# Softmax weights and queries in two PSUM banks, six banks for matmuls, in a gated attention and Mish kernel

## The chip, the cores and the metric

The kernel runs on one core of a Trainium2 chip. The metric is the device time of one execution in microseconds (us). TensorE does the matmuls (PE in the profile's rows; PEld are its weight loads), VectorE (DVE), ScalarE (ACT) and GpSimd (POOL) the elementwise work, SyncE (SP) issues most DMAs.

## What is computed

A row of x (2048 rows of 640) is gated by its own sigmoid g between two branches: sliding, dilated attention over 8 keys with 32 heads of 20, and a two-layer MLP with Mish and 1728 hidden columns. All arrays are float32.

```python
g = sigmoid((x * gate_w).sum(-1, keepdims=True))
# A: W, dil = 8, 2; key and value rows pos, pos-2, ..., pos-14 (masked below 0)
logits = einsum("bhsd,bhswd->bhsw", q, kg) * Dh ** -0.5
attn = softmax(where(mask, logits, -1e9))
a = einsum("bhsw,bhswd->bhsd", attn, vg).transpose(...).reshape(B, S, D) @ wo
# B
h = einsum("bsd,df->bsf", x, w1) + b1
b = einsum("bsf,fd->bsd", h * tanh(softplus(h)), w2)
return g * a + (1 - g) * b
```

## The kernel before

**Matmuls.** Every float32 operand of a matmul is split into a rounded high part (ScalarE, a copy to fp32r) and the low rest, raw minus high (a subtraction on VectorE or GpSimd, `split`, line 348; its output is a tile called `pair`). A product is three matmuls (`mm3`, lines 394 to 396): high by high, high by low, low by high. For part of the weights, the rest is instead made by a DMA of GpSimd's queue that adds in memory (`split_added`, line 357). The second MLP layer and half of the output projection use a scheme with seven block products in place of eight; its sums of blocks are made on VectorE or GpSimd (`sums_of`, lines 751 and 764) or by accumulating DMAs of GpSimd's queue (lines 657 and 1066).

**Attention** is not done with matmuls. It works in 8 units (4 groups of 8 heads by 2 halves of the rows); `kv` holds keys and values of a unit, slot by slot, and `q` its queries. For two slots at a time VectorE multiplies q by the window of 8 keys (`scores`, line 451, into `pr`, 2560 elements in each partition), reduces over the 20 columns of a head (line 454), and after the softmax multiplies the values by the weights `pw` (`outputs`, line 488), and adds up over the 8 keys in three halving steps (lines 493, 494, 496). Softmax runs on four slots: maximum, subtraction, Exp on ScalarE (line 473), sum, reciprocal, gate, weights (line 482). Masks are small ScalarE copies (line 463). The result is transposed by 32-blocks on VectorE (line 407), stored, and read again as operand of the output projection.

**Stages.** q, k and v come from matmuls into PSUM that ScalarE copies out (lines 552, 554, 556); between the units' matmuls run those of the first MLP layer with Mish on ScalarE (line 669); then the second layer (`mlp2`), the output projection of the first half of the rows (`wo_first`), and that of the last two token blocks (`wo_second`). In `wo_second` a column block's matmuls come in two parts, an opening part over three row blocks of the operand and a closing one over two. When a group is done, VectorE adds the gated MLP result to the bank (`finish`, line 1282); the MLP results are gated by a multiplication (line 943), some after a load from memory.

**Order.** Nothing is left to run-time choice. Each step is a task with an engine, an estimated duration, a rank and buffers from rings (PSUM `bank`: 8, `pair`: 21, `raw` and others). `Plan.run` plays the tasks through with these estimates and writes the instructions of each engine in the order in which they start. Subtractions and sums marked "ANY" are done by GpSimd or VectorE: VectorE takes one only when it is due, GpSimd any that is ready. From the first attention task on, GpSimd may begin such a task only if it ends by `quiet`, the estimated end of a running score reduction; the instruction is then also made to wait (`follow`) for the VectorE instruction before that reduction:

```python
if on:
    fit = [t for t in fit if now + t.ns[0] <= quiet + 150 or t.rank <= -0.5]
```

Of the kernel before, what the change touches and what calls it, by code (L numbers as in the profile page):

```python
# [8 lines left out]
F32 = mybir.dt.float32  # L9
F32R = mybir.dt.float32r  # L10
AF = mybir.ActivationFunctionType
OP = mybir.AluOpType
AX = mybir.AxisListType
PSUM = bass.MemoryType.PSUM
DRAM = bass.MemoryType.DRAM

S, D, H, DH, W, F = 2048, 640, 32, 20, 8, 1728
KC = D // 128
NQ, HQ = 4, 8
QF = HQ * DH  # L20
# [6 lines left out]
BIG = 1e9  # L27
WARM, WARM_TAIL = 6, 4
WA = 256

# [27 lines left out]
class Plan:  # L60


    NEAR, PATIENCE = 8000, 2000

    LAG = {"PE": 220, "ACT": 220, "DVE": 200, "POOL": 150, "SP": 3000}
    FAR, ROOM = 25000, 5000
# [29 lines left out]
    def run(self):  # L96
        ready = {e: [] for e in self.LAG}
# [4 lines left out]
        quiet, gate, last, shared, begun = 0.0, None, None, [], False  # L102
# [33 lines left out]
        while left:  # L136
            again = not events or events[0][0] > now
            while again:
                again = False
                for e in self.LAG:  # L140
                    if busy[e]:
                        continue
                    fit = [t for t in ready[e] if fits(t)]
                    on = begun and loud
                    if e == "POOL":
                        fit += [t for t in shared if fits(t)]
                        if on:
                            fit = [t for t in fit if now + t.ns[0] <= quiet + 150 or t.rank <= -0.5]
                    elif e == "DVE":
                        fit += [t for t in shared if fits(t) and (not on or due(t))]  # L150
                    if not fit:
                        continue
                    t = min(fit, key=lambda t: t.key)
                    if t.both:
                        shared.remove(t)
                        t.eng = e
                    else:
                        ready[e].remove(t)
                    if type(t.ns) is tuple:
                        t.ns = t.ns[e == "DVE"]  # L160
                    for b in t.take:
                        b.ring.free -= 1
                        b.ring.at += 1
                        b.t = b.make()
                    t.start = now
                    ins = t.fn(e) if t.both else t.fn()
                    if e == "POOL" and on and quiet > now and gate and ins:
                        self.follow(ins, gate)
                    if e == "DVE":
                        if t.kind:  # L170
                            begun = True
                            loud -= 1
                        if t.kind == "qk sum":
                            quiet, gate = now + t.ns, last
                        last = ins or last
                    if e == "PE":
                        begun_pe = max(begun_pe, t.pos)
                    busy[e] = again = True
                    end = over = now + t.ns * self.CARE.get(e, 1.0)
                    heapq.heappush(events, (over, n, "idle", e))  # L180
                    if t.land:
                        wire = max(wire, end) + t.land
                        end = wire + (0 if e == "SP" else self.ADDING)
                    heapq.heappush(events, (end + self.LAG[e], n + 1, "done", t))
                    if e != "SP":
                        heapq.heappush(events, (over, n + 2, "own", t))
                    n += 3
            if not events:
                stuck = [(t.eng, t.rank, t.waits, getattr(t.fn, "__qualname__", "")) for e in ready for t in ready[e]]
                raise RuntimeError(f"nothing can go on at {now}, {left} left: {stuck[:20]}")  # L190
            now, _, what, x = heapq.heappop(events)
            if what == "idle":
                busy[x] = False
                continue
            if what == "ready":
                (shared if x.both else ready[x.eng]).append(x)
                continue
            if what == "done":
                left -= 1
                x.at = now  # L200
                for b in x.hold:
                    b.left -= 1
                    if not b.left:
                        b.ring.free += 1
                        if b.gone:
                            b.gone()
            for t in x.then:

                if (t.eng == x.eng and x.eng != "SP") != (what == "own"):
                    continue  # L210
                t.waits -= 1
                if not t.waits:
                    t.why, t.rdy = x, now
                    late = self.ROOM if x.eng == "SP" and t.eng == "ACT" and first[t] - begun_pe > self.FAR else 0
                    heapq.heappush(events, (now + max(t.late, late), n, "ready", t))
                    n += 1
# [4 lines left out]
def kernel(ctx: ExitStack, tc: tile.TileContext, x, wq, wo, w1, b1, w2, xt, gw, out):  # L221
    nc = tc.nc
    scale = DH ** -0.5
    V, G, A = nc.vector, nc.gpsimd, nc.scalar

    keep = ctx.enter_context(tc.tile_pool(name="keep", bufs=1))
    dram = ctx.enter_context(tc.tile_pool(name="dram", bufs=1, space=DRAM))
    psum = ctx.enter_context(tc.tile_pool(name="psum", bufs=8, space=PSUM))
    top = ctx.enter_context(tc.tile_pool(name="top", bufs=1, side="right"))
    pe = ctx.enter_context(tc.tile_pool(name="pe", bufs=1, side="right"))  # L230
    at = ctx.enter_context(tc.tile_pool(name="at", bufs=1))
# [1 line left out]
    NPAIR, NW, NRAW, NH = 21, 3, 7, 4  # L233
    def follow(ins, gate):
        tc.add_manual_dep(ins.ins, gate.ins.name,
                          mybir.DependencyInfo(mybir.DependencyClass.Sync, mybir.DependencyReason.DATA), reason="beside")

    plan = Plan({"bank": 8, "pair": NPAIR, "w": NW, "raw": NRAW, "raw1": 1, "hb": NH,
                 "ot": 1, "b": 11}, follow)

    def ps_buf():
# [23 lines left out]
    def act_ns(n):  # L265
        return 30 + 0.96 * n
# [13 lines left out]
    add = plan.add  # L280
# [36 lines left out]
    lg_w = lg.rearrange("p s h w -> p s w h")  # L317
    pw = at.tile([128, 8, W, HQ], F32, name="pw")
    pw_h = pw.rearrange("p s w h -> p s h w")
    pr = at.tile([128, 2, W, QF], F32, name="pr")  # L320
    mx = at.tile([128, 8, HQ], F32, name="mx")
    sm = at.tile([128, 8, HQ], F32, name="sm")
# [99 lines left out]
    def window(kv, s0, which):  # L422
        a = kv[:, s0:s0 + 9, which, :]
        return bass.AP(tensor=a.tensor, offset=a.offset, ap=[list(a.ap[0]), [ROW, 2], [ROW, W], [1, QF]])
# [6 lines left out]
    def attention(u, P, hq, ready, gates):  # L431


        kv, q = KV[UNIT[u]], Q[UNIT[u]]
# [13 lines left out]

        def scores(s0, rank, after):
            def mul():  # L450
                return V.tensor_tensor(pr, window(kv, s0, 0), q[:, s0:s0 + 2, None, :].to_broadcast([128, 2, W, QF]), op=OP.mult)  # L451

            def red():
                V.tensor_reduce(lg_w[:, s0:s0 + 2], pr.rearrange("p s w (h d) -> p s w h d", d=DH), op=OP.add, axis=AX.X)  # L454

            step = chain(rank)
            step("DVE", 2850, mul, ready[s0] + after, kind="qk")
            return step("DVE", 2750, red, kind="qk sum")

        def bounded(a, b, after):  # L460
# [15 lines left out]
        def shares(a, rank, e, copied):  # L476
            h = slice(a, a + 4)
            step = chain(rank)
            t = step("DVE", 415, lambda: V.tensor_reduce(sm[:, h], lg[:, h], op=OP.add, axis=AX.X), [e])
            step("DVE", 390, lambda: V.reciprocal(sm[:, h], sm[:, h]))  # L480
            step("DVE", 230, lambda: V.tensor_tensor(sm[:, h], sm[:, h], gate[:, P, h, None].to_broadcast([128, 4, HQ]), op=OP.mult), gates)
            return t, step("DVE", 430, lambda: V.tensor_tensor(pw[:, h], pw[:, h], sm[:, h, None, :].to_broadcast([128, 4, W, HQ]), op=OP.mult), [copied])

        def outputs(s0, rank, after):
            def mul():
                vw = window(kv, s0, 1)
                vw = bass.AP(tensor=vw.tensor, offset=vw.offset, ap=[list(d) for d in vw.ap[:3]] + [[DH, HQ], [1, DH]])
                V.tensor_tensor(pr.rearrange("p s w (h d) -> p s w h d", d=DH), vw,  # L488
                                pw[:, s0:s0 + 2, :, :, None].to_broadcast([128, 2, W, HQ, DH]), op=OP.mult)

            step = chain(rank)
            step("DVE", 2850, mul, after, kind="pv")
            step("DVE", 1495, lambda: V.tensor_tensor(pr[:, :, 0:4], pr[:, :, 0:4], pr[:, :, 4:8], op=OP.add), kind="pv")  # L493
            step("DVE", 855, lambda: V.tensor_tensor(pr[:, :, 0:2], pr[:, :, 0:2], pr[:, :, 2:4], op=OP.add), kind="pv")

            return step("DVE", 525, lambda: V.tensor_tensor(q[:, s0:s0 + 2], pr[:, :, 0], pr[:, :, 1], op=OP.add), kind="pv")
# [16 lines left out]
        for i, a in enumerate((4, 0)):  # L513
            h = 2 * u + i
# [938 lines left out]
```

## Time and profile before

| | us |
|---|---|
| timed runs | 632.35, 631.42, 631.64 |
| median | 631.64 |
| profiled execution: span from first to last instruction | 630.2 |
| busy TensorE, VectorE | 625.6, 581.0 |
| busy ScalarE, GpSimd | 333.5, 143.4 |

The profiled execution's own time is told by its span alone; the timed runs stand 1.2 to 2.2 us above that span. A row of the groups reads: line, engine, operation, output<-inputs by the program's names, shapes, count, then busy time in us and mean ns of one, then the engine's idle time just before and what ended it. A row of the timeline reads: start in us, duration in us, engine, line, operation, names, shapes, count, with the idle time before it in brackets. A row of the waits reads: who, for whom, us in total, times, the longest.

### The profile page before, as it was taken

What the parts mean: (1) busy time and instruction counts of PE and PEld (TensorE: products, weight loads), DVE (VectorE), ACT (ScalarE), POOL (GpSimd) and SP (SyncE); (2) the same over time, 40 slices, a digit from 0 to 9 for tenths busy, and PEclk for the clock granted to TensorE, in tenths of its full rate; (3) what the DMA queues carried; (4) which work ended last, traced back from release to release, by engine and by line L of the source; (5) the groups of instructions that cost most, each with busy time, mean ns of one, the idle gap of its engine ahead of it and who ended that gap; (6) DMA issues with size and microseconds to landing.
All of it is one profiled execution on the core that took longest, in us unless ns stands there. A gap on an engine that the chain in (4) does not pass through costs nothing.

```text
span 630.2 us, 8823 instructions
## 1 busy us (share of the span) xinstructions
PE 625.6 (99%) x2794; PEld 521.9 (83%) x2794; DVE 581.0 (92%) x610; ACT 333.5 (53%) x705; POOL 143.4 (23%) x154
## 2 busy tenths in 40 slices
PE   9999999999999999999999999999999999999997
PEld 6888888888888888888888888888888888888886
DVE  7699989999999998998999899999999989999934
ACT  6665764454536645353652626683765536666300
POOL 1321242232312332331333341211201010002320
PEclk9999999999999999999999999999999999999999
DMA  9999998999977998895898798899989867799985
GB/s 321 344 338 225 180 271 210 317 256 274 269 206 175 322 313 195 209 271 112 186 324 185 150 290 196 216 322 287 298 275 287 231 222 252 231 340 322 253 236 189
DMA packets 105694, 159.12 MB, mean 253 GB/s; under 512 B 13728, under 2 KB 52768, under 8 KB 105360
## 3 DMA queue, kind: packets, MB, share of 16 engines
q1 hardware_dynamic: 89648, 131.74, 64.1%
q0 software_dynamic: 15712, 26.56, 27.3%
q8 instruction: 22, 0.36, 0.2%
q10 hardware_dynamic: 288, 0.26, 0.1%
q14 instruction: 24, 0.20, 0.1%
HBM read 95.27 MB, written 67.51 MB: 258 GB/s over the span
## 4 chain that ended last, share of the span: by engine, by line
PE 98%; DMA 1%; ACT 0%; SPq 0%; DVE 0%; issue 0%
PE bank L395 32%; PE bank L394 32%; PE bank L396 32%; DMA hb<-in_x 1%; PE bank L400 1%; PE bank L401 1%; PE bank L546 0%; SPq L362 0%; ACT kvq L345 0%; ACT pair L345 0%; DVE kvq L1282 0%
## 5 line engine op out<-in xcount | busy, mean ns | idle before, releaser
L395 PE MATMUL bank<-pair 128*128 128x512 f32 (+1 forms) x500 | 193.1, 386 | 0.0
L394 PE MATMUL bank<-pair 128*128 128x512 f32 (+1 forms) x500 | 193.1, 386 | 0.0
L396 PE MATMUL bank<-pair 128*128 128x512 f32 (+1 forms) x500 | 193.1, 386 | 0.0
L396 PEld LDWEIGHTS bank<-pair 128*128 128x128 f32 x500 | 93.9, 188 | 18.1
L394 PEld LDWEIGHTS bank<-pair 128*128 128x128 f32 x500 | 93.9, 188 | 18.1
L395 PEld LDWEIGHTS bank<-pair 128*128 128x128 f32 x500 | 93.9, 188 | 17.9
L488 DVE TENSOR_TENSOR pr<-kvq,pw 128x2560 f32<-128x2560 f32 x32 | 91.7, 2865 | 1.0
L451 DVE TENSOR_TENSOR pr<-kvq 128x2560 f32<-128x2560 f32 x32 | 91.0, 2843 | 0.9
L454 DVE TENSOR_REDUCE lg<-pr 128x128 f32<-128x2560 f32 x32 | 90.2, 2819 | 0.7
L345 ACT ACTIVATE pair<-raw 128x512 fp32r<-128x512 f32 (+3 forms) x120 | 70.5, 611 | 33.4 <-DMA raw<-o 18.1
L552 ACT ACTIVATE kvq<-bank 128x320 f32<-128x320 f32 x64 | 28.0, 438 | 82.9 <-PE bank L396 82.4
L394 PE MATMUL bank<-pair,w 128*128 128x512 f32 x182 | 70.8, 389 | 0.0
L395 PE MATMUL bank<-pair,w 128*128 128x512 f32 x182 | 70.8, 389 | 0.0
L396 PE MATMUL bank<-pair,w 128*128 128x512 f32 x182 | 70.8, 389 | 0.0
L348 DVE TENSOR_TENSOR pair<-raw,pair 128x512 fp32r<-128x512 f32 (+2 forms) x103 | 67.1, 678 | 2.7 <-ACT pair L345 2.6
L669 ACT ACTIVATE hb<-bank,bias 128x512 f32<-128x512 f32 x52 | 35.6, 688 | 59.2 <-PE bank L396 55.7
L395 PE MATMUL bank<-pair,kvq 128*128 128x496 f32 (+2 forms) x149 | 56.4, 378 | 0.0
L394 PE MATMUL bank<-pair,kvq 128*128 128x496 f32 (+2 forms) x149 | 56.4, 378 | 0.0
L396 PE MATMUL bank<-pair,kvq 128*128 128x496 f32 (+2 forms) x149 | 56.4, 378 | 0.0
L345 ACT ACTIVATE pair<-hb 128x512 fp32r<-128x512 f32 (+3 forms) x62 | 37.9, 611 | 23.8 <-DMA hb<-actt 12.3
L657 POOL DMA_DIRECT2D actt<-actt x28 | 26.7, 965 | 95.7 <-DMA actt<-actt 53.5
L493 DVE TENSOR_TENSOR pr<-pr 128x1280 f32<-128x1280 f32 x32 | 47.5, 1486 | 0.3
(130 smaller groups left out, 896.8 us busy)
## 6 DMA issues: line engine op xcount, KB each, us to landing
actt<-hb SPq DMA_DIRECT2D x52, 256.0 KB, 6.3
act<-hb SPq DMA_DIRECT2D x38, 256.0 KB, 6.1
raw<-actt SPq DMA_DIRECT2D x35, 256.0 KB, 4.1
raw<-act SPq DMA_DIRECT2D x30, 256.0 KB, 4.9
actt<-hb POOLq DMA_DIRECT2D x26, 256.0 KB, 6.8
actt<-actt POOLq DMA_DIRECT2D x24, 256.0 KB, 6.0
kvq<-in_xt SPq DMA_DIRECT2D x16, 320.0 KB, 7.0
o<-ot SPq DMA_DIRECT2D x64, 80.0 KB, 4.3
```

Source lines behind the costliest of these rows:

```text
L345: a = add("ACT", act_ns(n), lambda: A.activation(hi(), raw(), AF.Copy), after, rank=rank, take=take, hold=hold)
L348: return (V if e == "DVE" else G).tensor_tensor(lo(), raw(), hi().bitcast(F32), op=OP.subtract)
L394: nc.tensor.matmul(ps, ah, bh, start=first, stop=False, skip_group_check=more)
L395: nc.tensor.matmul(ps, ah, bl, start=False, stop=False, skip_group_check=more)
L396: nc.tensor.matmul(ps, al, bh, start=False, stop=last, skip_group_check=more)
L451: return V.tensor_tensor(pr, window(kv, s0, 0), q[:, s0:s0 + 2, None, :].to_broadcast([128, 2, W, QF]), op=OP.mult)
L454: V.tensor_reduce(lg_w[:, s0:s0 + 2], pr.rearrange("p s w (h d) -> p s w h d", d=DH), op=OP.add, axis=AX.X)
L488: V.tensor_tensor(pr.rearrange("p s w (h d) -> p s w h d", d=DH), vw, pw[:, s0:s0 + 2, :, :, None].to_broadcast([128, 2, W, HQ, DH]), op=O ...
L493: step("DVE", 1495, lambda: V.tensor_tensor(pr[:, :, 0:4], pr[:, :, 0:4], pr[:, :, 4:8], op=OP.add), kind="pv")
L552: a = add("ACT", 330, lambda: A.activation(kv[:, 7 + s], ps.t[:, QF:3 * QF].rearrange("p (a b) -> p a b", a=2), AF.Copy), [done] + before, ...
L657: return add("POOL", 1200, lambda: G.dma_start(out=blk[key][:rows], in_=src(), accum_op=OP.add, max_dma_last_dim=2048), after, rank=-0.5, ...
L669: a = add("ACT", 595, lambda: A.activation(to(it()), src(), AF.Mish, bias=bias[:n, fc:fc + 1]), after + [bias_in], rank=NEXT, take=[] if h ...
```

## The change

PSUM's eight banks are divided: six stay with the matmuls, one holds `pg`, the softmax weights of all eight slots of a unit, and one `qg`, the queries of two slots. ScalarE copies q of two slots to `qg` ahead of each product, and the next copy waits for the product that reads `qg`. The weights are written to `pg` by the multiplication that wrote `pw`. So either product has one operand in PSUM and one in SBUF. `QUIET` lets GpSimd's tasks begin beside both products as well as beside the score reduction.

```diff
+NBANK = 6
+    QUIET = ("qk", "qk sum", "pv mul")
...
-                        if t.kind == "qk sum":
+                        if t.kind in self.QUIET:
                             quiet, gate = now + t.ns, last
...
-    psum = ctx.enter_context(tc.tile_pool(name="psum", bufs=8, space=PSUM))
+    psum = ctx.enter_context(tc.tile_pool(name="psum", bufs=NBANK, space=PSUM))
+    shared = ctx.enter_context(tc.tile_pool(name="shared", bufs=1, space=PSUM))
...
-    plan = Plan({"bank": 8, "pair": NPAIR, "w": NW, "raw": NRAW, "raw1": 1, "hb": NH,
+    plan = Plan({"bank": NBANK, "pair": NPAIR, "w": NW, "raw": NRAW, "raw1": 1, "hb": NH,
...
+    pg = shared.tile([128, 8, W, HQ], F32, name="pg")
+    qg = shared.tile([128, 2, QF], F32, name="qg")
+    qg_free = [None]
...
-                return V.tensor_tensor(pr, window(kv, s0, 0), q[:, s0:s0 + 2, None, :].to_broadcast([128, 2, W, QF]), op=OP.mult)
+                return V.tensor_tensor(pr, window(kv, s0, 0), qg[:, :, None, :].to_broadcast([128, 2, W, QF]), op=OP.mult)
...
-            step("DVE", 2850, mul, ready[s0] + after, kind="qk")
+            c = add("ACT", act_ns(2 * QF), lambda: A.activation(qg, q[:, s0:s0 + 2], AF.Copy), ready[s0] + [qg_free[0]], rank=-1)
+            qg_free[0] = step("DVE", 2850, mul, ready[s0] + after + [c], kind="qk")
...
-            return t, step("DVE", 430, lambda: V.tensor_tensor(pw[:, h], pw[:, h], sm[:, h, None, :].to_broadcast([128, 4, W, HQ]), op=OP.mult), [copied])
+            return t, step("DVE", 430, lambda: V.tensor_tensor(pg[:, h], pw[:, h], sm[:, h, None, :].to_broadcast([128, 4, W, HQ]), op=OP.mult), [copied])
...
-                                pw[:, s0:s0 + 2, :, :, None].to_broadcast([128, 2, W, HQ, DH]), op=OP.mult)
+                                pg[:, s0:s0 + 2, :, :, None].to_broadcast([128, 2, W, HQ, DH]), op=OP.mult)
...
-            step("DVE", 2850, mul, after, kind="pv")
+            step("DVE", 2850, mul, after, kind="pv mul")
```

The planner works with the new rings and rules, so the orders of the engines change in many places.

## The prediction

> **What bounds the kernel now.** I read the first page first (busy shares, chain), then who waited for whom on TensorE and on its weight loads, then the busy time by stretches.
>
> ```profile
> PE 625.6 (99%) x2794; PEld 521.9 (83%) x2794; DVE 581.0 (92%) x610; ACT 333.5 (53%) x705; POOL 143.4 (23%) x154
> PE 98%; DMA 1%; ACT 0%; SPq 0%; DVE 0%; issue 0%
> ```
>
> ```profile
> PE bank L330 <- PEq L1441: 0.8, 1, 0.8
> PE bank L573 <- DVE pair L1323: 0.3, 1, 0.3
> PE bank L546 <- ACT pair L345: 0.2, 1, 0.2
> ```
>
> ```profile
> 0.00:10.00 10.00, 8.67 (x34) 5.65 (x35) 6.84 (x11) 5.26 (x8) 2.25 (x6) 1.00 0.83 274
> 10.00:300.00 290.00, 290.00 (x1300) 243.79 (x1299) 274.45 (x248) 158.29 (x360) 77.96 (x83) 1.00 0.97 252
> 300.00:600.00 300.00, 300.00 (x1332) 249.81 (x1331) 288.25 (x338) 168.67 (x337) 59.32 (x63) 1.00 0.90 256
> 600.00:627.00 27.00, 26.90 (x133) 22.69 (x131) 11.05 (x16) 1.26 (x2) 3.92 (x4) 1.00 0.70 221
> 627.00:630.20 3.20, 0.00 (x0) 0.00 (x0) 0.36 (x1) 0.00 (x0) 0.00 (x0) 1.00 0.45 164
> ```
>
> ```profile
> 604.77 0.39 PE L394 MATMUL bank<-pair,kvq 128*128 128x512 f32 x1
> 606.81 0.39 PE L394 MATMUL bank<-pair,kvq 128*128 128x512 f32 x1
> 608.85 0.39 PE L394 MATMUL bank<-pair,kvq 128*128 128x512 f32 x1
> ```
>
> The columns of the fence by stretches are stretch, its length, and then the busy time of TensorE, weight loads, VectorE, ScalarE and GpSimd, the granted clock, the DMA share and GB/s. TensorE has no idle time from 10 to 600 us, and its only three listed waits are at the lines of the first stage. Busy time alone could hide gaps, since a 512-wide matmul is drawn 0.39 us long (last fence: start, duration); the count tells: 1332 matmuls in 300 us is one per 0.2252 us, and back-to-back ones start every 0.2267 us at 512 columns (18 of them between 604.77 and 608.85) and slightly sooner at 496. So the order of matmuls is issued without a hole, at clock 1.00. VectorE at 92% is the second busiest, but nobody on the chain waits for it.
>
> What is not matmul: 1.33 us in the first 10, 0.10 before 627 and 3.20 after, 4.63 together, which is 630.20 less 625.57. The span is 630.2 us and the median of the timed runs 631.64; the 1.5 us between them lie outside the span, and I add them to every span below.
>
> **The change part by part.** *TensorE.* The order of the changed program has the same 2794 matmuls with the same operands until the last 25 us, where 60 places differ: with six banks the output projection of the last two token blocks can't open eight at once, so the closing halves of two groups come ahead of the opening halves of two others. Added work there: none. Sum: 0.
>
> *VectorE and GpSimd.* 57 subtractions and sums go from VectorE to GpSimd (45 there before, 102 after), 41 of them 512 wide, the rest mostly narrower. The two products read one operand from PSUM.
>
> ```profile
> L488 DVE TENSOR_TENSOR pr<-kvq,pw 128x2560 f32<-128x2560 f32 x32 | 91.7, 2865 | 1.0
> L451 DVE TENSOR_TENSOR pr<-kvq 128x2560 f32<-128x2560 f32 x32 | 91.0, 2843 | 0.9
> L348 DVE TENSOR_TENSOR pair<-raw,pair 128x512 fp32r<-128x512 f32 x88 | 59.4, 697 | 2.7 <-ACT pair L345 2.6
> L1282 DVE TENSOR_TENSOR raw<-bank,raw 128x512 f32<-128x512 f32 x5 | 3.5, 692 | 13.5 <-PE bank L396 13.5
> L552 ACT ACTIVATE kvq<-bank 128x320 f32<-128x320 f32 x64 | 28.0, 438 | 82.9 <-PE bank L396 82.4
> L348 POOL TENSOR_TENSOR pair<-hb,pair 128x512 fp32r<-128x512 f32 x4 | 5.3, 1323 | 31.5 <-DMA kvq<-in_xt 22.2 <-DVE zt L626 9.2
> ```
>
> VectorE sheds at most 57 x 0.70 = 40 us; with the widths as they are about 36. GpSimd gains at most 57 x 1.32 = 75 us and stands near 215 of 630. Whether the 64 products get dearer is not shown for this shape; the nearest row is L1282, an add with one operand in PSUM, at 692 ns beside 697 for one with both in SBUF, so I take 0. For the ends I use the 22 ns by which the two products differ among themselves: 64 x 0.022 = 1.4 us more or less. It would lie on VectorE, under TensorE's stream. [...]
>
> The point of the edit is which VectorE instructions GpSimd can run beside. The trace has both kinds:
>
> ```profile
> 599.53 2.40 DVE L943 TENSOR_TENSOR kvq<-kvq,w 128x512 f32<-128x512 f32 x1
> 599.76 1.61 POOL L943 TENSOR_TENSOR hb<-hb,w 128x512 f32<-128x512 f32 x1
> ```
>
> ```profile
> 610.62 1.30 POOL L943 TENSOR_TENSOR raw<-raw,w 128x512 f32<-128x512 f32 x1
> 611.77 0.69 DVE L1282 TENSOR_TENSOR raw<-bank,raw 128x512 f32<-128x512 f32 x1 [0.67 <-PE bank L396]
> ```
>
> With both operands in SBUF, VectorE's multiplication took 2.40 us where 0.69 is usual, and GpSimd 1.61 in place of 1.30. With one operand in PSUM, the add took its usual 0.69 although GpSimd's was running. So the products should leave GpSimd alone, as the edit wants.
>
> *ScalarE.* 32 copies of q into PSUM; the nearest row is L552, the same 320 columns, 438 ns: 14 us, from 333 to 347 of 630. Beside other work throughout, as long as the wait discussed below stays short. The 16 multiplications that now write the weights to PSUM have no such row; by the same 22 ns either way they are within 0.4 us of VectorE's time, hidden as well: 0.
>
> *Banks.* I followed every one of the 160 bank tenancies through the timeline. In the trace of before never more than six are open at once, but for the groups that begin at 604.77 and 606.81. Giving each group the bank it has in the changed program, the tightest reuse ahead of the last 25 us is this:
>
> ```profile
> 124.63 0.19 ACT L556 ACTIVATE hx<-bank 128x16 f32<-128x16 f32 x1
> 129.21 0.38 PE L394 MATMUL bank<-pair,kvq 128*128 128x496 f32 x1
> ```
>
> Emptied at 124.82, wanted at 129.21: 4.4 us spare. Cost: 0. In the last 25 us:
>
> ```profile
> 593.33 0.69 DVE L348 TENSOR_TENSOR pair<-raw,pair 128x512 fp32r<-128x512 f32 x1
> 595.80 0.69 DVE L348 TENSOR_TENSOR pair<-hb,pair 128x512 fp32r<-128x512 f32 x1
> 610.41 0.69 DVE L1282 TENSOR_TENSOR raw<-bank,raw 128x512 f32<-128x512 f32 x1 [8.47 <-PE bank L396]
> ```
>
> The closing group that begins at 608.85 is six matmuls (1.36 us); its add starts 1.56 after the group and ends 2.25 after it. In the new order that group starts at 604.77, its bank is free at 607.02; a second closing group fills TensorE until 607.49, and only then is the bank wanted: 0.47 us spare. The next has 1.15. The last operand of that closing group was split by 596.49 in before (second row), 8.3 us ahead of its new start. Cost: 0, with the smallest margin of the whole change.
>
> *Readiness of the split operands.* The tightest after the first 14 us:
>
> ```profile
> 562.79 0.68 DVE L348 TENSOR_TENSOR pair<-raw,pair 128x512 fp32r<-128x512 f32 x1
> 566.69 0.39 PE L394 MATMUL bank<-pair,kvq 128*128 128x512 f32 x1
> ```
>
> 3.2 us. A subtraction moved to GpSimd takes 0.63 us more (1.32 less 0.69), so 2.6 are left even there. Sum over the change: 0 on the path, hidden by TensorE's unbroken stream. The span stays 630.2, the time 631.7.
>
> **The rivals.**
>
> *ScalarE is held at the new copies (slower).* The copy for the second slot pair waits until VectorE has read the first from the only q tile; behind it in ScalarE's order stand Mish activations and evacuations, which empty banks, and the rounding copies of splits, for which VectorE and TensorE wait. Before has one wait of this kind, the mask activations:
>
> ```profile
> ACT lg L463 <- DVE lg L454: 19.7, 7, 6.2
> POOL actt L657 <- DMA actt<-actt: 53.5, 9, 7.7
> ```
>
> ```profile
> 514.29 1.29 POOL L348 TENSOR_TENSOR pair<-raw,pair 128x512 fp32r<-128x512 f32 x1
> 522.71 0.39 PE L394 MATMUL bank<-pair 128*128 128x512 f32 x1
> ```
>
> The copies' model is the first row (total, times, longest): 2.8 us each, the longest 6.2. From a hold above 3.2 us, with an operand due behind it, TensorE stops: 6.2 less 3.2 is 3.0 us, so 634.7 for one such place, 633.5 where a bank (4.4) is what waits. Against it: seven holds already stopped nothing, and a VectorE with 36 us less to do runs less late. GpSimd's order has the same weakness: a subtraction beside a product is made to wait for the VectorE instruction ahead of it, and subtractions and accumulating DMAs, which waited up to 7.7 us (second row), stand behind each other; but the closest split that it made in before was ready at 515.58 and read at 522.71, 7.1 us later.
>
> *The last stage loses its margin (slower).* The add at 607.02 stands behind VectorE's gate multiplications for the last block (L943); their loads stand in SP's queue behind stores of results that wait for GpSimd's accumulation.
>
> ```profile
> 596.40 0.84 DVE L407 STREAM_TRANSPOSE ot<-kvq 128x640 f32<-128x640 f32 x1
> 606.04 0.90 SPq L362 DMA_DIRECT2D raw<-b  x2
> raw<-actt SPq DMA_DIRECT2D x35, 256.0 KB, 4.1
> raw<-act SPq DMA_DIRECT2D x30, 256.0 KB, 4.9
> ```
>
> Each microsecond that the last of these loads is late past 0.47 is a microsecond of the end. Landing 4.1 to 4.9 us after issue, as loads of that size do, and gated in 0.7, it must be issued by about 601. If it went out as late as 606.04, the end is some 4.4 us later: 636. Against it: the last of their buffers comes from a split that was done at 594.02 in before (the row at 593.33), VectorE idled 8.47 us ahead of the first such add, and the last attention transpose, here at 596.40, moves from instruction 588 of 607 to 470 of 553, which empties this stage further.
>
> *It does not do what it says.* If GpSimd and the products still shut each other out, each moved subtraction costs VectorE the 1.7 us of the L943 pair: 581 - 36 + 57 x 1.7 = 642 us of work, VectorE becomes the bound, 643 or more. The PSUM add beside GpSimd speaks against it. [...]
>
> *Faster.* 36 us less on VectorE could pay only where TensorE waits for operands: 0.5 us at L573 and L546, where instructions and order are untouched, and the tail after the last matmul, whose two adds and stores stay. At most 0.5 us, 631.1, which counts as no change.
>
> **How the numbers follow.** No effect, the small gain included, 0.68; ScalarE or GpSimd order 0.14; last stage 0.11; locks 0.04; 0.03 for faster by more, by a cause that I don't see in the rows. A difference under 0.2%, 1.26 us, is about what cannot be told from no change here (the three runs spread 0.93). The forecast is the likeliest case, 631.7, alone 631.0 to 632.5. The range goes down to 630.9 and up to 634.7, the priced hold; the late load at 636 and the locks stay out. Chances: faster 0.03, same 0.68, slower 0.29.
>
> **What would show it.** Right: TensorE again full in every stretch from 10 to 600 us, its waits only in the first 8; VectorE's busy time near 545; GpSimd's near 215; the products at 2.82 to 2.9 us also beside GpSimd; ScalarE near 347 and its copies of q waiting for VectorE under 3 us. Wrong: any wait of TensorE on a pair or a bank after 10 us, first of all near 607; products well over 3 us; a span not at 630 with TensorE full, which would mean slower matmuls, a thing nothing here shows.

## The result and the profile after

The changed kernel takes 634.59 us in the median of seven runs (634.14 to 639.96), against 631.64 for the kernel before (631.32 to 632.54): a ratio of 1.0061 with an interval of 1.0038 to 1.0085. It is slower by 0.6%, where no change was forecast. The profiled execution is one of 634.59 us; its span is 632.8 us, 2.6 more than the 630.2 of before, and 1.8 us lie outside it.

The busy time and the chain of the page, and below them all of TensorE's waits:

```profile
PE 626.7 (99%) x2794; PEld 522.7 (83%) x2794; DVE 570.9 (90%) x553; ACT 342.2 (54%) x737; POOL 217.9 (34%) x211
PE 97%; DMA 1%; ACT 0%; issue 0%; DVE 0%; SPq 0%
```

```profile
PE bank L401 <- ACT kvq L1171: 1.9, 1, 1.9
PE bank L337 <- PEq L1449: 0.8, 1, 0.8
```

GpSimd has gained 75 us and stands at 217.9, near the 215 expected. VectorE has shed only 10 of the 36. And TensorE has one new wait of 1.9 us, for a ScalarE copy (line 1171, line 1163 of before). The view by stretches puts it between 300 and 600 us, where TensorE had been busy without a hole:

```profile
10.00:300.00 290.00, 290.00 (x1300) 243.73 (x1299) 271.56 (x238) 164.78 (x379) 88.87 (x95) 1.00 0.98 251
300.00:600.00 300.00, 298.09 (x1323) 247.82 (x1322) 284.34 (x293) 171.85 (x350) 123.60 (x107) 1.00 0.89 260
600.00:627.00 27.00, 27.00 (x129) 22.72 (x128) 5.76 (x9) 0.00 (x0) 3.14 (x4) 1.00 0.65 160
627.00:632.90 5.90, 2.52 (x17) 2.13 (x15) 2.00 (x4) 0.00 (x0) 0.00 (x0) 1.00 0.47 175
```

The granted clock is 1.00 throughout, so matmuls did not get slower; nine fewer were run between 300 and 600 us, at 0.2267 us each about 2.0 us. The timeline gives the gap itself: two matmuls start 2.30 us apart where 0.227 is the pitch, 2.07 us lost. The rest of the 2.6 us, some 0.5, lies in the first 10 us and in slight slips after the gap.

**Followed back from the gap.** The chain of waits runs through it like this (start, duration, what ended last):

```profile
570.03 0.47 issue
570.50 1.15 ACT pair L352 x2
571.65 0.69 DVE pair L355
572.35 0.33 SPq L813
572.74 0.48 SPq L813
573.32 5.69 DMA hb<-o
579.07 0.49 issue
579.69 0.40 issue
580.09 0.59 ACT kvq L1171
580.72 0.50 PE bank L401
```

Read from below: the matmul at 580.72 adds onto a bank that ScalarE first has to copy out (580.09). In ScalarE's order the rounding copy of a block (579.03) stands ahead of that copy, and the block's load landed only at 579.01. That load was issued at 573.32, because in SP's order a pair of loads (572.35 and 572.74) stands ahead of it, which went out only when VectorE's subtraction of 571.65 had freed a staging buffer. That subtraction in turn began as ScalarE's rounding copies (570.50) ended, and these stood behind a copy out of a bank that TensorE had just filled. In ScalarE's rows of the timeline the hold is the bracket:

```profile
579.03 0.63 ACT L352 ACTIVATE pair<-hb 128x512 fp32r<-128x512 f32 x1 [2.01 <-DMA hb<-o]
579.57 0.61 ACT L352 ACTIVATE pair<-raw 128x512 fp32r<-128x512 f32 x1
580.09 0.58 ACT L1171 ACTIVATE kvq<-bank 128x512 f32<-128x512 f32 x1
```

So the last subtraction on the chain was not late by VectorE's own doing. The subtractions just before it were, as the rows of VectorE and GpSimd show:

```profile
560.72 3.31 POOL L355 TENSOR_TENSOR pair<-raw,pair 128x512 fp32r<-128x512 f32 x2
566.44 4.73 POOL L355 TENSOR_TENSOR pair<-hb,pair 128x512 fp32r<-128x512 f32 x3 [0.70 <-ACT pair L352]
566.81 1.78 DVE L355 TENSOR_TENSOR pair<-hb,pair 128x512 fp32r<-128x512 f32 x1
568.52 6.90 DVE L355 TENSOR_TENSOR pair<-raw,pair 128x512 fp32r<-128x512 f32 x7
```

Subtractions that take VectorE 0.69 us take up to 1.78 while GpSimd has one of its own (the row at 566.81; the first two of the seven at 568.52 take 1.78 and 1.50), and GpSimd's take 1.6 in place of 1.3. Both read two operands from SBUF. That is the pair of rows at line 943 which the prediction showed, 2.40 and 1.61 us, and the price which the change was to avoid. Each of these three slowed subtractions held back a load: SP issued the next one within 0.03 us of its end. Meanwhile the DMA share (the last but one number of a row by stretches) fell from 0.97 to 0.37:

```profile
568.62 0.32 SPq L369 DMA_DIRECT2D hb<-so  x1
570.32 0.32 SPq L369 DMA_DIRECT2D raw<-so  x1
571.75 0.32 SPq L369 DMA_DIRECT2D raw<-o  x1
```

```profile
564.00:568.00 4.00, 4.00 (x20) 3.30 (x19) 4.00 (x4) 3.96 (x9) 3.29 (x3) 1.00 0.97 338
568.00:572.00 4.00, 4.00 (x19) 3.34 (x18) 4.00 (x4) 3.03 (x6) 4.00 (x5) 1.00 0.37 115
```

The loads that followed went out close together, and the one of 573.32 took 5.69 us, where the median of its kind is 5.1 (4.9 in before). That the slowed subtractions made this load late is a reading of these rows; how much of the 2.0 us came in that way, and how much by ScalarE's place in its order, the trace alone does not tell. The experiments tell whether the wait is there without GpSimd's sums.

**Why they met.** The planner keeps GpSimd's tasks beside VectorE instructions that they hardly slow (the score reduction takes 2818 ns beside a GpSimd sum in before, 2821 without one) only while attention tasks remain: the condition is `on = begun and loud`, and `loud` counts the products, score reductions and halving sums that VectorE has yet to begin. The last of them began at 594.8 us in before and at 526.0 here. The transpose of the last result, which follows, stood at 596.40 in before and stands 64 us earlier here:

```profile
531.90 0.83 DVE L414 STREAM_TRANSPOSE ot<-kvq 128x640 f32<-128x640 f32 x1
```

The relief itself brought the end of attention forward, and with it the end of the rule. From then on GpSimd takes any task that is ready, and VectorE too takes one that is not yet due. The same 72 us, first of before and then of after:

```profile
528.00:600.00 72.00, 72.00 (x319) 59.63 (x318) 69.61 (x108) 41.35 (x73) 10.40 (x13) 1.00 0.95 278
```

```profile
528.00:600.00 72.00, 70.09 (x310) 57.69 (x309) 63.74 (x75) 39.71 (x73) 41.74 (x32) 1.00 0.92 287
```

GpSimd has 32 instructions in place of 13. VectorE has 75 for 108, but one of them takes 850 ns in the mean, where it was 645. I counted, over the trace, each VectorE instruction with a GpSimd sum beside it, and what it took above the median of its own form without one: after 528 us GpSimd does 22 sums, 19 VectorE instructions are slowed, and 17.0 us are lost. Over the whole kernel it is 29.7 us, against 10.1 in before, of which 1.7 after 528 us.

### The profile page after: what moved, and what is told of

Read it like the earlier page. It is cut to its first block, busy times and chain, and to the rows that moved or that the text cites. A ratio compares the mean times of both kernels' runs of the same rounds, so it can differ in the third digit from the quotient of the medians.

```text
span 632.8 us, 8912 instructions
## 1 busy us (share of the span) xinstructions
PE 626.7 (99%) x2794; PEld 522.7 (83%) x2794; DVE 570.9 (90%) x553; ACT 342.2 (54%) x737; POOL 217.9 (34%) x211
## 4 chain that ended last, share of the span: by engine, by line
PE 97%; DMA 1%; ACT 0%; issue 0%; DVE 0%; SPq 0%
PE bank L401 32%; PE bank L403 32%; PE bank L402 32%; PE bank L554 1%; DMA hb<-o 1%; PE bank L408 1%; PE bank L407 1%; DMA raw<-in_wq 0%; ACT pair L352 0%; SPq L813 0%; DVE pair L355 0%; ACT kvq L1171 0%; PE bank L581 0%; DVE kvq L1290 0%; SPq L369 0%
## 5 line engine op out<-in xcount | busy, mean ns | idle before, releaser
L458 DVE TENSOR_TENSOR pr<-kvq,qg 128x2560 f32<-128x2560 f32 x32 | 90.0, 2812 | 3.3 <-ACT pair L363 1.4
L496 DVE TENSOR_TENSOR pr<-kvq,pg 128x2560 f32<-128x2560 f32 x32 | 90.2, 2819 | 1.0
L461 DVE TENSOR_REDUCE lg<-pr 128x128 f32<-128x2560 f32 x32 | 90.2, 2818 | 0.9
L355 POOL TENSOR_TENSOR pair<-raw,pair 128x512 fp32r<-128x512 f32 (+1 forms) x40 | 54.1, 1369 | 45.6 <-ACT pair L352 18.1
L355 DVE TENSOR_TENSOR pair<-raw,pair 128x512 fp32r<-128x512 f32 (+2 forms) x80 | 63.8, 825 | 4.8 <-ACT pair L352 4.7
L665 POOL DMA_DIRECT2D actt<-hb x26 | 25.2, 993 | 80.3 <-ACT hb L677 33.5
```

Source lines behind the costliest of these rows:

```text
L355: return (V if e == "DVE" else G).tensor_tensor(lo(), raw(), hi().bitcast(F32), op=OP.subtract)
L458: return V.tensor_tensor(pr, window(kv, s0, 0), qg[:, :, None, :].to_broadcast([128, 2, W, QF]), op=OP.mult)
L665: return add("POOL", 1200, lambda: G.dma_start(out=blk[key][:rows], in_=src(), accum_op=OP.add, max_dma_last_dim=2048), after, rank=-0.5, ...
```

## The experiments

Two theories stood at first. One: the rule lapses, and in the last stage instructions of GpSimd and VectorE that read two operands from SBUF lengthen one another, which makes the wait (the texts call this lengthening, and the theory, the locks). The other: six banks, or the copies of q on ScalarE, make it.

**The rule kept to the end.**

```diff
-                    on = begun and loud
+                    on = begun
```

> The changed kernel, but the rule that lets GpSimd begin a subtraction only within the planned time of a product or a score reduction stays in force after the last attention instruction (before, and in the change, it ends there). GpSimd then has none of the 22 sums that it ran after 528 us in the changed kernel, of which 19 slowed a VectorE instruction, by 17.0 us together. Locks theory (GpSimd and two-SBUF VectorE instructions shut each other out after attention, staging buffers come free late, loads are late, ScalarE waits for them ahead of a bank's copy): TensorE's 2 us wait near 580 us is gone, 631.7 us (631.2 to 632.3), VectorE's slowed instructions after 528 us none. Six banks theory, or the theory that ScalarE is held at the copies of q: the wait stays, 634 to 635. Late loads theory (the loads land late whatever GpSimd does): the wait stays, 633.5 or more.

Measured: 632.29 us, ratio 1.0004 (0.9994 to 1.0014), in the profiled execution, the shortest of eleven (630.89 to 633.51), a span of 629.1. TensorE's only wait is that of the start, and the last stage is this:

```profile
PE bank L337 <- PEq L1449: 0.8, 1, 0.8
```

```profile
528.00:600.00 72.00, 72.00 (x319) 59.61 (x318) 56.26 (x94) 38.48 (x71) 10.51 (x12) 1.00 0.96 291
```

No GpSimd sum lies beside anything after 528 us. VectorE does 19 instructions more than in after and needs 7.5 us less for them (599 ns each). The products still have both operands as the change put them, the banks are six, the copies of q are there, and attention ends as early as in after (the last transpose at 524.1 us): the loss is gone with this edit alone. The edit does two things, though. It takes GpSimd's sums away after attention, and it keeps VectorE from taking a sum before it is due; the run with idle sums below keeps the second and puts the first back.

**Six banks alone**, on the kernel before.

```diff
+NBANK = 6
-    plan = Plan({"bank": 8, ...
+    plan = Plan({"bank": NBANK, ...
```

> The kernel before with six banks in its ring and nothing else. Six banks theory: TensorE waits for a bank or a copy out of one, 633.5 to 635. Locks theory and the copies theory: no wait after the first 10 us, 631.7 us (631.2 to 632.3).

Measured: 631.76 us, ratio 1.0 (0.9992 to 1.0009), TensorE's waits again only those of the start. Two banks fewer cost nothing.

**Everything but the wider windows**, on the kernel after: GpSimd may begin beside score reductions alone, as in before.

```diff
-    QUIET = ("qk", "qk sum", "pv mul")
+    QUIET = ("qk sum",)
```

> The changed kernel with its two PSUM tiles, six banks and 32 copies of q, but GpSimd may begin only beside the score reduction, as before. The attention then ends about as late as before (the last transpose is instruction 559 of 573 on VectorE). Locks theory: hardly any GpSimd sums after attention, no wait of TensorE after 10 us, 631.7 us (631.2 to 632.3). Copies theory (ScalarE held at the copies of q) and six banks theory: a wait of 1 us or more, 633 to 635.

Measured: 631.91 us, ratio 0.9999 (0.999 to 1.0008), no wait of TensorE after the start. Attention ends as late as before (in the trace the last transpose is instruction 592 of 612, at 595.5 us; the expectation's count was off). So the copies of q, the operands in PSUM and the six banks together cost nothing either. What costs comes with the wider windows: GpSimd's larger share ends attention early, and the rule with it.

**The rule ended early, on the kernel before.** If it is the end of the rule, it should hurt there too, with eight banks and no copy of q.

```diff
-                    on = begun and loud
+                    on = begun and loud > 9
```

The condition holds only until nine of the counted attention tasks are left; in the trace GpSimd's sums run beside anything from about 521 us on.

> The kernel before (eight banks, no operand of the products in PSUM, no copies of q), but the rule on GpSimd is lifted when nine attention instructions are left, about 527 us in the trace of before. Locks theory: GpSimd runs a score of sums after that beside two-SBUF VectorE instructions, VectorE loses 10 us or more there, and TensorE waits 1 us or more after 527 us: 632.7 to 636. Theories of banks and of copies: nothing of theirs is in it, 631.7 us (631.2 to 632.3).

Measured: 648.11 us, ratio 1.0256 (1.0242 to 1.027), far more than either theory had put on record; the direction is that of the lapsed rule, the size is not. TensorE waits for splits:

```profile
PE bank L395 <- POOL pair L348: 6.4, 1, 6.4
PE bank L395 <- DVE pair L348: 4.9, 2, 4.7
```

In the whole of this kernel VectorE loses 33.5 us beside GpSimd. The longest wait is for a split that GpSimd made itself, after it had been busy without a break from 547 us on. So this run shows that the early end of the rule hurts with eight banks and without the copies of q; it does not separate lengthened VectorE instructions from GpSimd's own late results. The two long waits are 11.1 of the 16.5 us by which the span grew (646.7 for 630.2); most of the rest is told with the hardware below.

**Locks alone.** To the kernel with the rule kept, 22 subtractions of GpSimd on `pr`, which is free after attention, were added; what they write is not used. All other engines keep their orders, but for two neighbouring VectorE instructions that changed places near 596 us.

```diff
-                    on = begun and loud
+                    on = begun
...
+    for i in range(22):
+        idle = add("POOL", 1329, lambda: G.tensor_tensor(flat[:, :512], flat[:, 512:1024], flat[:, 1024:1536], op=OP.subtract),
+                   [idle], rank=-0.55, late=1500)
```

> The kernel with the rule kept, and 22 more GpSimd subtractions after the last attention instruction, 512 wide, on a tile that nobody reads any more; each waits for a VectorE instruction, so that they are spread, and nobody waits for them. The orders of the other engines stay instruction for instruction. Locks theory (VectorE's instructions lengthened by GpSimd's are enough): 10 to 17 us of VectorE lost after 528 us, and TensorE waits 0.5 us or more after 540 us: 632.3 to 636. Theory of the slow server (the change loses time because results that TensorE needs are made by GpSimd at 1.3 us and behind its DMAs, not because of locks): 631.7 us (631.2 to 632.3), no wait after 10 us.

Measured: 635.38 us, ratio 1.0056 (1.0044 to 1.0068).

```profile
PE bank L404 <- DVE pair L357: 2.2, 4, 0.9
```

```profile
528.00:600.00 72.00, 69.81 (x303) 56.23 (x303) 71.79 (x84) 38.89 (x71) 38.66 (x28) 1.00 0.87 256
```

Idle work of GpSimd, 21 sums of it behind 528 us, takes 21.5 us from VectorE there, TensorE waits for splits four times (2.2 us), and the time is that of the change within the intervals. No needed result comes from these sums and no buffer was bound: the locks suffice for a loss of this size. They make it by other waits than in the change, four short ones for splits in place of one for a copy out of a bank.

**A wider rule without PSUM**, on the kernel before: GpSimd may begin beside the products, whose operands both stay in SBUF.

```diff
-                        if t.kind == "qk sum":
+                        if t.kind in ("qk", "qk sum", "pv mul"):
```

> The kernel before, eight banks and both operands of the products in SBUF, but GpSimd may begin beside the products too (the wider rule alone). If operands in SBUF are what shuts GpSimd out: products with a GpSimd sum beside them take 3.5 us or more in place of 2.82, VectorE's sheds little of its 581 us, and with the rule lapsing after attention TensorE waits as in the change or longer: 633 to 640. If the PSUM operands do nothing: products at 2.82 us, and a time like the change's, 634 to 635.

Measured: 664.55 us, ratio 1.0514 (1.0499 to 1.053). The way was not the expected one: the products hardly suffer (line 451: 2896 ns in the mean of all, 2989 beside a GpSimd sum, 2815 without one); GpSimd does. A subtraction of 512 columns beside a product takes it 2946 ns (19 of them), beside the products of the change 1340 (24 of them). First the GpSimd subtractions of this kernel, then those of after:

```profile
L348 POOL TENSOR_TENSOR pair<-raw,pair 128x512 fp32r<-128x512 f32 x31 | 60.9, 1983 | 19.0 <-ACT pair L345 10.7 <-DVE pair L780 5.4 <-ACT kvq L923 1.3
```

```profile
L355 POOL TENSOR_TENSOR pair<-raw,pair 128x512 fp32r<-128x512 f32 x31 | 44.5, 1452 | 31.6 <-ACT pair L352 17.4 <-PE bank L403 7.9 <-DMA act<-w 3.1
```

TensorE's waits for GpSimd's late splits come to 7.4 us at one of its lines and 7.1 at another. The operands in PSUM do what they are for: GpSimd and the products no longer slow each other.

**The planner told of the locks**, on the kernel after: after attention, a shared task is estimated 1.25 times as long on GpSimd, and a VectorE task begun meanwhile 700 ns longer.

```diff
+                    if begun and not loud and t.both and e == "POOL":
+                        end = over = now + 1.25 * t.ns
+                        shut = end
+                    if begun and not loud and e == "DVE" and now < shut:
+                        end = over = over + 700
```

> The changed kernel, with the planner's estimates after attention made longer, as the locks made the instructions: GpSimd's shared tasks by 1.25, VectorE's by 0.7 us while one of them runs. The rule still lapses after attention, GpSimd still works beside two-SBUF instructions. If it is the order written from too short estimates (a bank's copy behind a load that comes late) that stops TensorE: no wait after 10 us, 631.7 us (631.2 to 632.5), though VectorE still loses 10 us or more after 528 us. If it is the lost capacity itself: a wait of 1 us or more, 633 to 636.

Measured: 633.77 us, ratio 1.0044 (1.0022 to 1.0066), with twelve runs between 632.44 and 638.86. The profiled execution, one of the four at 638 us and more, has a wait of 3.9 us for a VectorE split, and VectorE loses 27 us after 528 us: the order was planned with the locks and has more of them, since GpSimd is given still more (54 us busy between 528 and 600, for 42 in after). The eight shorter runs (632.44 to 634.25) have no trace. This run is inconclusive. It shows that these longer estimates don't reliably remove the wait, not how much of it is due to estimates that were too short.

None of these versions beats the kernel before: the order of matmuls is full there, and where the loss is taken away, the time is that of before.

## Why the prediction was wrong

**The bound, and that nothing could be gained: right.** Every version that leaves TensorE full came out within 0.1% of before, with VectorE's busy time anywhere from 562 to 581 us.

**Matmuls and banks: right.** Six banks alone cost nothing, and the smallest margin named, at the end of `wo_second`, held: from 600 to 627 us TensorE is full. The bank behind the wait at 580 us was one that TensorE went on adding to, not a new one that it wanted.

**The products: right.** These are the groups of after:

```profile
L458 DVE TENSOR_TENSOR pr<-kvq,qg 128x2560 f32<-128x2560 f32 x32 | 90.0, 2812 | 3.3 <-ACT pair L363 1.4
L496 DVE TENSOR_TENSOR pr<-kvq,pg 128x2560 f32<-128x2560 f32 x32 | 90.2, 2819 | 1.0
```

2812 and 2819 ns stand against 2843 and 2865 in before. Beside a GpSimd sum they take as long as alone (2813 and 2811 for the first, 2816 and 2820 for the second), so the rival that the locks stay for the products is out. The means of before hide something that the working overlooked: one product of line 451 and three of line 488 already lay beside a GpSimd sum there and took 3724 ns and 3259 ns in the mean, the others 2814 and 2824. So most of the 22 ns between the two products came from a few disturbed ones, and the lower means of after are the end of that, not a faster read from PSUM.

**The copies of q: right.** The copies take the 14 us that were summed; ScalarE's busy time has only 8.7 us more, because it counts the overlapping ends of neighbouring instructions once (47.5 us of overlap for 42.4 in before). ScalarE was held at them for 13.4 us in all and never longer than 3.0, and the version that has the copies without the wider windows has no wait of TensorE.

```profile
L464 ACT ACTIVATE qg<-kvq 128x320 f32<-128x320 f32 x32 | 14.1, 441 | 13.5 <-DVE pr L458 13.4
```

**VectorE and GpSimd: wrong by its size.** The 57 subtractions were credited at 36 us; 10 were shed. The term took the moved instructions at their undisturbed price on both engines, and their neighbours on VectorE at their old one. GpSimd's sum, near 215 us, came out at 217.9. What was missing is the neighbours: they lost 19.6 us more than in before (29.7 less 10.1). That leaves 16.4 of the 36, and VectorE's durations, added up one by one, did fall by 16.9 (609.7 to 592.8). The busy time fell by 10 because it counts overlapping ends once, and with 57 instructions fewer there is less overlap (21.9 us for 28.7). That neighbours were slowed shows in the mean of VectorE's split of 512 columns:

```profile
L355 DVE TENSOR_TENSOR pair<-raw,pair 128x512 fp32r<-128x512 f32 x67 | 57.1, 874 | 4.3 <-ACT pair L352 4.2
```

In before it was 697 ns. Without a GpSimd sum beside it a split of 512 columns takes 680 in after, with one 1230 (78 and 30 of them, counting both those that read `raw` and those that read `hb`).

**"Readiness of the split operands ... hidden by TensorE's unbroken stream": the step that failed.** It took before's tightest margin, 3.2 us, and asked only how much longer one subtraction takes on the slower engine. It did not ask where the moved subtractions would lie. What the runs showed in its place: after 528 us 22 of GpSimd's sums lay beside VectorE instructions with two operands in SBUF, these lost 17.0 us, and TensorE stopped for 1.9 us; without those sums the wait is gone (632.29 us), and with as many idle ones put back the loss is too (635.38). The wait was not for a split made by the slower engine but for a copy out of a bank, held behind a late load. The working had all that was needed: the price of two operands in SBUF beside GpSimd (the line 943 rows, used there for the products), the sentence that the last transpose moves from instruction 588 of 607 to 470 of 553, and the planner's code. The part on the order says from when GpSimd's rule holds, but not until when. That earlier transpose was read as relief for the last stage; it was also a sign of the end of the rule. The line `on = begun and loud` was not read for what it does when `loud` comes to zero early. The splits, too, have both operands in SBUF: beside a GpSimd sum they took 1230 ns for 680.

**The rivals.** "ScalarE is held at the new copies" had the right last link, ScalarE held ahead of a copy that empties a bank, and a price that fits: 633.5 to 634.7 against 634.59. Its cause was not the one: the hold is a late load, and the copies of q don't make it. That the price fits is luck. "Locks" were tied to the products and to VectorE becoming the bound; they came elsewhere, where 17 us are enough. "The last stage loses its margin" did not occur. Of the signs named for being wrong, "any wait of TensorE on a pair or a bank after 10 us" was the one that came, at 578 to 581 us, and not near 607.

**What stays open.** How far the wait is due to estimates that are too short, and how far to capacity that is lost whatever is planned, was not told apart. That slowed subtractions made the load late, and by how much, is read from one trace and was not tested by itself. Only one execution of the change was profiled; those at 636.08 to 639.96 us are not explained by its trace, though the last section gives a likely part of it.

## What to carry to other kernels

When a change relieves an engine, look for every condition in the scheduler that ends with that engine's work: an earlier end moves the point at which the condition lapses, and what it kept apart then meets. Cost a moved instruction by what lies beside it at its new place, on both engines, rather than by its own duration. A margin read from the old order holds only for the stage as it was filled then.

## What the runs showed of the hardware

**A wait of TensorE can cost more than its length.** In the kernel before with the rule ended early, 512-wide matmuls after the waits start every 0.427 us in place of 0.227, and the granted clock fell with them:

```profile
558.19 0.79 PE L395 MATMUL bank<-pair 128*128 128x512 f32 x1 [6.42 <-POOL pair L348]
558.78 0.63 PE L396 MATMUL bank<-pair 128*128 128x512 f32 x1
565.84 0.79 PE L395 MATMUL bank<-pair 128*128 128x512 f32 x1 [4.72 <-DVE pair L348]
571.55 0.48 PE L396 MATMUL bank<-pair 128*128 128x512 f32 x1
572.09 0.39 PE L395 MATMUL bank<-pair 128*128 128x512 f32 x1
```

```profile
566.00:568.00 2.00, 2.00 (x5) 1.61 (x6) 2.00 (x3) 0.00 (x0) 0.64 (x1) 0.50 0.57 172
572.00:574.00 2.00, 2.00 (x11) 1.65 (x10) 1.97 (x2) 1.10 (x4) 0.99 (x1) 1.00 0.92 318
```

The clock is 0.50 from 566 to 570 us and 1.00 again from 572, with matmuls one per 0.427 us for 5.7 us after the second wait: some 19 slow ones in all, at 0.2 us more 3.8 us, and with the waits 14.9 of the 16.5. In the planner's version, after a wait of 3.9 us, the slow matmuls begin 1.4 us after its end and last 3.3 us, with a granted clock of 0.74 in the mean from 579 to 583 us:

```profile
579.80 0.50 PE L407 MATMUL bank<-pair 128*128 128x512 f32 x1 [3.86 <-DVE pair L360]
581.18 0.63 PE L406 MATMUL bank<-pair 128*128 128x512 f32 x1
584.50 0.39 PE L408 MATMUL bank<-pair 128*128 128x512 f32 x1
```

After the 1.9 us of the change the clock stayed at 1.00 (580.7 to 585 us). But the length of one wait does not decide. In the version with the wider rule and no operand in PSUM (granted clock 0.982 in the mean of the execution) the clock stood at 0.50 also behind a wait of 2.31 us and behind one of 1.10 us with two of 0.2 after it. The two cases and the stretches behind them:

```profile
462.23 0.50 PE L395 MATMUL bank<-pair 128*128 128x512 f32 x1 [2.31 <-POOL pair L348]
588.03 0.50 PE L394 MATMUL bank<-pair 128*128 128x512 f32 x1 [1.10 <-ACT pair L345]
```

```profile
464.00:467.00 3.00, 3.00 (x8) 2.33 (x8) 3.00 (x3) 1.43 (x3) 2.74 (x3) 0.50 0.94 317
590.20:593.20 3.00, 3.00 (x8) 2.32 (x8) 3.00 (x5) 2.79 (x6) 3.00 (x3) 0.50 0.89 307
```

So a wait of 1.10 us was followed by the lower clock, and the 1.9 us of the change was not. What sets the fall off was not shown.

Spells of the lower clock would also explain part of the scatter: the four runs of the planner's version at 638 us and more have a granted clock of 0.994 to 0.997, the eight others 0.999 or 1.000, and of the change's runs those at 639.96 and 636.08 have 0.995 and 0.997. The run at 636.47 has 1.000, so that is not all of it.

**The other engine can be the one that pays.** Beside products with both operands in SBUF, GpSimd's subtraction took 2946 ns in place of 1340, and the product 2989 in place of 2815; beside GpSimd's subtractions VectorE's short splits took 1230 ns for 680. A price read from one pair of instructions, as the prediction did, is not one for another pair.
